# The last stage of a fused attention and mixture kernel: A and B formed by halves of the columns, and a new layout of the work around it

## The chip, the cores and the metric

One core of one Trainium2 chip runs the whole kernel as one program. The metric is device time in microseconds (us), the median over runs of the same kernel. A core has TensorE (PE, matmuls; its weight loads are shown as PEld), VectorE (DVE), ScalarE (ACT), GpSimd (POOL) and SyncE (SP, which issues the DMAs here). Each engine works through its own queue in order and waits on semaphores.

## The reference

Causal attention gives x, a soft mixture of experts turns x into 32 slots, and the slots are combined per token with weights c. Then comes the last layer:

```python
def _moe2_ref(x, w_a, w_b, w_out):
    a = x @ w_a                     # x: 896 x 768, w_a, w_b: 768 x 1536
    b = x @ w_b
    return (a * b @ w_out)          # w_out: 1536 x 768
```

Since x = c @ slots, row i of a * b is a sum over pairs of slots (s, u) of c_s c_u times A_s * B_u, where A = slots @ w_a and B = slots @ w_b. The kernel forms the products of pairs of slots once (P), multiplies them with w_out (M), forms c_s c_u for all tokens (cc), and multiplies cc with M to get the output.

## The kernel before, in words

All work up to about 280 us is the same in both kernels. The pairs of slots are cut into five tiles of up to 128 pairs (`TILES`). Tiles 0 and 1 are done in earlier stages beside the experts, tile 4 (a small one, 16 pairs) is called M4. The last stage, when the last slots are known, does this:

- `fold_a`, `fold_b` (matmuls `fp`, copy `sT`) bring the new slots into place.
- `ab_chunk(q, c)` multiplies the slots with w_a (q = 0) or w_b (q = 1). One chunk is one sixth of the contraction for all 1536 columns, as four matmuls to four groups of 32 rows of one PSUM bank; `ab_copy` and `ab_turn` (ACT, three transposes on PE, ACT) bring the result into `abt`, with the 1536 columns as 12 blocks f of 128 partitions.
- `p_tile(k, ...)` makes P for pair tile k in cuts of 2 or 3 blocks f (`PCUTS`): `products` on DVE (`pt`, `pf`: two multiplications for each part of the tile and an addition), then `conv_p` splits the sum into a high half (ACT) and a low half (DVE). Each product needs A and B of its block.
- `w_late` splits blocks of w_out into high and low halves in the same way (`whl`; ACT and DVE); four blocks, f = 8 to 11, are left from the stage before (`wt`).
- `m_late(k)` is 12 blocks of six matmuls each (`m_mats`, tiles `M`), in the order of `FLATE`, for tiles 2 and 3. `m_split` splits the result (`ml` for tiles 0 and 1, `mhl` for 2 and 3).
- `m4_mats`, `m4_copy`, `m4_fold` (tiles `M4`, `mc`, `M4f`, `m`) do tile 4.
- `cc_step(n, k)` forms cc for 256 tokens n and one or two pair tiles: matmuls `c` on PE, ACT copy and DVE multiplication (`gt`), ACT rounding and a subtraction on POOL (`cc`).
- `o_mats(t, k)` are the output matmuls (tiles `o`) of 128 tokens t with pair tile k; `o_store` copies and sends them.

The order on each engine is the order in which the program issues the instructions. The table `TAIL` sets it: after each unit of the stage, and after each block of `m_late` and each `o_mats`, `gap()` takes so many units from the queues W (`w_late`), S (`m_split`), P (products), C (`cc_step`) and X (M4) as the table has at that spot. What a later step needs and the table has not taken yet is taken just ahead of it. In the kernel before the products can be taken only when `turned` is set, after the whole stage:

```python
for i, u in enumerate(stage()):
    u()
    gap()
turned.append(1)
gap()
```

Of the kernel before, what the change touches and what calls it, by code (L numbers as in the profile page):

```python
# [19 lines left out]
S = 448  # L20
# [7 lines left out]
for _i in range(7):  # L28
# [62 lines left out]
def moe_kernel(ctx: ExitStack, tc: tile.TileContext, pk, vt, phi, w1, w2, wab, wo, rsel, out):  # L91
# [413 lines left out]
    with tc.manual_schedule():  # L505
# [262 lines left out]
        abt = r2.tile([128, 2, 12, NSLOT], F32, name="abt")  # L768
# [18 lines left out]
        def ab_turn(q):  # L787
            ps = psM.tile([128, 3, 4, NSLOT], F32, tag="m", name=f"abt{q}")
            for j in range(3):
                nc.tensor.transpose(  # L790
                    ps[:, j].rearrange("p g s -> p (g s)"), ab_sb[q][:, 128 * j:128 * j + 128], ident
                )
            nc.scalar.activation(
                out=abt[:, q].rearrange("p (g j) s -> p j g s", j=3), in_=ps, func=AF.Copy
            )
# [3 lines left out]
        def products(p, k, lo, w):  # L799
            f = slice(lo, lo + w)  # L800
            jobs = []
            off = 0
            for kind, *v in TILES[k]:
                if kind == "rect":
                    i, n, u, m = v
                    jobs.append((off, (n, m), [
                        (abt[:, q, f, i:i + n].unsqueeze(3).to_broadcast([128, w, n, m]),
                         abt[:, 1 - q, f, u:u + m].unsqueeze(2).to_broadcast([128, w, n, m])) for q in range(2)
                    ]))
                    off += n * m  # L810
                elif kind == "tri":
                    e, n = v
                    g = [abt[:, q, f].rearrange("p f (e r) -> p f e r", r=4)[:, :, e:e + n] for q in range(2)]
                    for r in (1, 2, 3):
                        jobs.append((off, (n, r), [
                            (g[q][:, :, :, r:r + 1].to_broadcast([128, w, n, r]), g[1 - q][:, :, :, 0:r])
                            for q in range(2)
                        ]))
                        off += n * r
                else:  # L820
                    i, n = v
                    jobs.append((off, (n, 1), [
                        (abt[:, 0, f, i:i + n].unsqueeze(3), abt[:, 1, f, i:i + n].unsqueeze(3))
                    ]))
# [21 lines left out]
        def p_tile(k, place, cuts, rot=0):  # L846
# [6 lines left out]
            at = [(rot + sum(cuts[:i])) % 12 for i in range(len(cuts))]  # L853
# [11 lines left out]

            q = [lambda: prod(0), lambda: conv_p(0), lambda: prod(1)]
# [93 lines left out]
        def m4_mats(h):  # L960
            if h == 0:
                mx[0] = two("so", "M4")
            for f0 in (0, 4, 8):
                for g in range(4):
                    f = f0 + g
                    nc.tensor.matmul(
                        mx[0][h][32 * g:32 * g + 32, 0:384], lhsT=mx["p"][:, f, :],
                        rhs=wo_sb[f // 2][:, f % 2, 384 * h:384 * h + 384],
                        start=(f < 4), stop=(f >= 8), skip_group_check=True,
                    )  # L970
# [30 lines left out]

        cu = combine_units()
# [16 lines left out]
        def w_late(j):  # L1019
            f, h = divmod(j, 2)  # L1020
            if h == 0 and f < 4:
                whl[f] = slot_tile(f"r{f}", F32R, f"whl{f}").rearrange("p (h q d) -> p h q d", h=2, q=2)
            elif h == 0 and f % 2 == 0:
                t = wabp.tile([128, 2, 2, 2, 384], F32R, tag=f"wab{f // 2 - 2}", bufs=1, name=f"whl{f}")
                whl[f], whl[f + 1] = t[:, 0], t[:, 1]
# [5 lines left out]
        def late_next():  # L1031
            if wl_j[0] < 16:
# [8 lines left out]
        def cc_step(n, k):  # L1041
# [18 lines left out]
            for q in range(2):  # L1060
                if n == 0:
                    ps = psA.tile([128, 2, 256], F32, tag=("so1", "so0")[q], name=f"c{q}_{n}_{k}")
                else:
                    ps = psM.tile([128, 2, 256], F32, tag="m", name=f"c{q}_{n}_{k}")
# [23 lines left out]
        def m_split(k):  # L1088
            if k < 2:
                if not mhl:  # L1090
# [17 lines left out]
        def p_next(k):  # L1108
            if not turned or (k == 3 and ptq[2]):
                return  # L1110
            if ptq[k] == [0]:
                ptq[k][:] = p_tile(k, ("t0", "t1") if k == 2 else "wab5", PCUTS[k], FLATE[0])
# [6 lines left out]
        def cc_next():  # L1119
            if ccq and (ccq[0][0] == 0 or done3 or ccq[0][0] == 1):  # L1120
# [12 lines left out]
        def split_next():  # L1133
            if splits:
                m_split(splits.pop(0))

        def gap():
            for name, take in (("W", late_next), ("S", split_next), ("P", p_any), ("C", cc_next), ("X", m4_next)):
                c = TAIL[name]
                for _ in range(c[spot[0]] if spot[0] < len(c) else 0):  # L1140
# [50 lines left out]
        def m_late(k):  # L1191
            for i, f in enumerate(FLATE):
                cuts = PCUTS[k]
                n = [c for c in range(len(cuts)) if sum(cuts[:c]) <= i][-1]
                while ptq[k] and (ptq[k] == [0] or len(ptq[k]) > p_left(k, n)):
                    p_any()
                if i == 0:
                    while k == 3 and len(m4_units) > 1:
                        m4_next()
                    mps[k] = two(("ab", "so")[k - 2], f"M{k}")  # L1200
                for h in range(2):
                    while f < 8 and wl_j[0] <= 2 * f + h:
                        late_next()
                    m_mats(k, i, f, h, whl[f][:, h, 0], whl[f][:, h, 1])
                gap()
# [5 lines left out]
        m_late(2)
        while len(m4_units) > 2:
            m4_next()
        m_split(2)
        m_late(3)
        done3.append(1)
# [82 lines left out]
```

## Time and profile before

| | us |
|---|---|
| median of three runs | 370.74 |
| lowest, highest run | 370.56, 374.9 |
| span of the profiled execution | 370.0 |

The profiled execution shows its own time only as the span, from its first to its last instruction; the median is 0.7 us above it. The last stage runs from about 280 us to the end. A timeline row merges instructions of one form; its length reaches from the first start to the last end, and matmuls overlap, so the pace is read from starts.

### The profile page before, as it was taken

To read this page: it belongs to the slowest core of one execution; us is meant where nothing else is said; L and a number is where in the kernel's file an instruction comes from. 1 tells how busy PE (TensorE), PEld (TensorE's weight loads), DVE (VectorE), ACT (ScalarE), POOL (GpSimd) and SP (SyncE) were. 2 spreads that over 40 slices of the span, in tenths; PEclk is the share of its full clock that TensorE was granted. 3 is DMA by queue.
4 is the path that set the end of the run, shared out by engine and by line. 5 is a ranking of instruction groups with operands and counts; after the bars stand their busy time and mean duration, and the time that the engine had idled before them with its cause. 6 is when DMAs were issued, how large, how long until landed. Compare 5 with 4: busy or idle time off the path is not lost.

```text
span 370.0 us, 6891 instructions
## 1 busy us (share of the span) xinstructions
PE 334.6 (90%) x2551; PEld 201.8 (55%) x2551; DVE 230.1 (62%) x620; ACT 202.0 (55%) x464; POOL 91.1 (25%) x128
## 2 busy tenths in 40 slices
PE   8897898989989978988988889999899889999996
PEld 5454454544544655343342346634565359899995
DVE  3689989999999962021025887507856669933121
ACT  2599999999999952103007445414546732422221
POOL 2457666667766510001000000000000110301110
PEclk9999989999999999999999989999999999999999
DMA  7677789998677787999999999778910000001222
GB/s 282 269 240 282 273 309 389 345 341 288 247 280 280 245 289 308 390 421 416 418 332 402 396 338 351 263 317 272 421 78 2 0 1 2 0 2 43 85 87 85
DMA packets 20224, 90.51 MB, mean 245 GB/s; under 512 B 2336, under 2 KB 5024, under 8 KB 20192
## 3 DMA queue, kind: packets, MB, share of 16 engines
q1 hardware_dynamic: 20192, 90.09, 65.2%
q8 instruction: 20, 0.33, 0.4%
q14 instruction: 12, 0.10, 0.1%
HBM read 87.33 MB, written 2.75 MB: 243 GB/s over the span
## 4 chain that ended last, share of the span: by engine, by line
PE 46%; ACT 27%; DVE 16%; issue 4%; DMA 3%; POOL 3%; ACTq 0%; POOLq 0%; DVEq 0%
ACT p L278 8%; PE o L1172 8%; PE M L891 8%; PE h L651 5%; PE so L692 4%; ACT raw L165 4%; PE ab L777 4%; ACT wab L164 4%; DVE pf L833 3%; ACT pT L314 3%; PE s L257 3%; DVE pt L832 3%; DMA raw<-in_wo_dram 3%; POOL p L294 3%; ACT wo L164 2%
## 5 line engine op out<-in xcount | busy, mean ns | idle before, releaser
L294 POOL TENSOR_SCALAR p<-p,rc 128x448 f32<-128x448 f32 (+6 forms) x84 | 69.2, 837 | 46.4 <-DVE rc L291 36.9
L257 PE MATMUL s<-qk 64*64 64x448 f32 (+6 forms) x336 | 48.5, 403 | 0.1
L1076 POOL TENSOR_TENSOR cc<-gt,cc 128x512 fp32r<-128x512 f32 (+1 forms) x6 | 6.9, 1156 | 157.6 <-ACT cc L1075 157.6
L278 ACT ACTIVATE p<-s,nm 128x448 f32<-128x448 f32 (+6 forms) x84 | 40.0, 492 | 7.8 <-DVE nm L268 7.6
L891 PE MATMUL M<-wt,P_t 128*128 128x384 f32 x168 | 35.9, 356 | 4.1 <-DVE P_t L864 1.3
L307 PE MATMUL t<-ident,p 128*128 128x128 f32 x192 | 33.7, 293 | 5.1 <-POOL p L294 5.1
L195 DVE SCALAR_TENSOR_TENSOR raw<-raw 128x768 int32<-128x768 int32 x36 | 35.2, 978 | 3.0 <-ACT raw L165 3.0
L263 DVE TENSOR_REDUCE nm<-s 128x1 f32<-128x448 f32 (+6 forms) x84 | 31.7, 411 | 8.0 <-PE s L257 8.0
L891 PEld LDWEIGHTS M<-wt,P_t 128*128 128x128 f32 x168 | 29.1, 193 | 13.6 <-ACT wt L885 4.8
L345 PE MATMUL v<-pT,v 128*64 128x448 f32 (+3 forms) x192 | 26.9, 396 | 7.9 <-ACT pT L314 7.7
L165 ACT ACTIVATE raw<-raw 128x768 int32<-128x768 uint32 x36 | 33.9, 941 | 0.0
L651 PE MATMUL h<-w,sT 128*32 128x512 f32 x192 | 29.9, 614 | 3.2 <-DMA w<-in_w_dram 2.3
L257 PEld LDWEIGHTS s<-qk 64*64 64x64 f32 x336 | 19.9, 136 | 21.3 <-issue 15.6
L307 PEld LDWEIGHTS t<-ident,p 128*128 128x128 f32 x192 | 20.7, 142 | 17.6 <-POOL p L294 7.3
L885 ACT ACTIVATE wt<-wo 128x384 fp32r<-128x384 f32 x48 | 21.8, 513 | 13.6 <-PE M L891 13.1
L886 DVE TENSOR_TENSOR wt<-wo,wt 128x384 fp32r<-128x384 f32 x48 | 23.8, 552 | 8.5 <-ACT wt L885 8.5
L198 DVE SCALAR_TENSOR_TENSOR wab<-wab,raw 128x768 int32<-128x768 int32 x24 | 27.9, 1162 | 0.8
L777 PE MATMUL ab<-wab,sT 128*32 128x384 f32 x288 | 27.5, 498 | 0.5 <-DVE sT L616 0.5
L692 PE MATMUL so<-w,hpad 128*32 128x384 f32 x256 | 24.8, 493 | 0.9 <-ACT wt L885 0.4
L314 ACT ACTIVATE pT<-t 128x512 f32<-128x512 f32 x35 | 21.7, 619 | 5.5 <-PE t L307 5.0
L345 PEld LDWEIGHTS v<-pT,v 128*64 128x64 f32 (+1 forms) x192 | 10.9, 134 | 22.6 <-ACT pT L314 14.0
L164 ACT ACTIVATE wab<-raw 128x768 f32<-128x768 f32 x24 | 23.1, 962 | 0.0
(155 smaller groups left out, 519.5 us busy)
## 6 DMA issues: line engine op xcount, KB each, us to landing
w<-in_w_dram SPq DMA_DIRECT2D x64, 768.0 KB, 8.0
raw<-in_wab_dram SPq DMA_DIRECT2D x24, 768.0 KB, 5.3
raw<-in_wo_dram SPq DMA_DIRECT2D x12, 768.0 KB, 4.4
qk<-in_pk_dram SPq DMA_DIRECT2D x12, 448.0 KB, 4.9
v<-in_pk_dram SPq DMA_DIRECT2D x12, 192.0 KB, 5.5
out_dram<-ost SPq DMA_DIRECT2D x6, 384.0 KB, 2.3
v<-in_vt_dram SPq DMA_DIRECT2D x12, 32.0 KB, 5.3
out_dram<-ost SPq DMA_DIRECT2D x2, 192.0 KB, 1.9
```

The lines of the kernel that those rows point to most:

```text
L164: nc.scalar.activation(out=dst, in_=hi, func=AF.Copy, scale=2.0 ** -112)
L165: nc.scalar.activation(out=pr[:, :, 0], in_=lw, func=AF.Copy, scale=2.0 ** -29, bias=-0.49999)
L195: nc.vector.scalar_tensor_tensor(out=b, in0=ph, scalar=-0x80000000, in1=b, op0=ALU.bitwise_and, op1=ALU.bitwise_or)
L257: nc.tensor.matmul(sb[r, o:o + n], lhsT=qT[r, 64 * i:64 * i + 64], rhs=kT[r, 0:n], start=False, stop=True, skip_group_check=True,)
L278: nc.scalar.activation(out=d["p"][:, POFF[i]:POFF[i] + n], in_=sb[:, o:o + n], func=AF.Exp, bias=d["nm"][:, c:c + 1], scale=d["scale"], ac ...
L294: nc.gpsimd.tensor_scalar(out=p[:, POFF[i]:POFF[i] + n], in0=p[:, POFF[i]:POFF[i] + n], scalar1=rc[:, CIX[i]:CIX[i] + 1], scalar2=1.0, op0 ...
L307: nc.tensor.transpose(ps[:, j, :], d["p"][:, o:o + 128], ident)
L345: nc.tensor.matmul(ps[r, 128 * kt:S], lhsT=lhsT, rhs=rhs, start=(kt == 0), stop=(kt == 3), skip_group_check=True)
L651: nc.tensor.matmul(ps[32 * g:32 * g + 32, :], lhsT=sT[:, 0, c, :], rhs=wt[8 * e + i // 3][:, 512 * (i % 3):512 * (i % 3) + 512], start=(i ...
L692: nc.tensor.matmul(so[32 * g:32 * g + 32, 0:384], lhsT=t[:, c, :], rhs=wt[8 * e + 4 + i // 4][:, 384 * (i % 4):384 * (i % 4) + 384], start ...
L777: nc.tensor.matmul(abps[q][32 * g:32 * g + 32, 0:384], lhsT=sT[:, 1, c, :], rhs=w[:, c % 2, 384 * g:384 * g + 384], start=(c == 0), stop=( ...
L891: nc.tensor.matmul(mps[k][h][:, 0:384], lhsT=l[:, f, :], rhs=r, start=(n == 0 and i == 0), stop=(n == 11 and i == 2))
```

## The change

A and B are no longer formed one after the other. `half_chunk(x, c)` multiplies one sixth of the contraction with 768 columns of both w_a and w_b (four matmuls, the same number and shape as before); half x = 0 covers blocks f = 6 to 11, half 1 blocks 0 to 5. Each half has its own copy and turn, and `turned` counts them. Products of tile 2 for blocks 6 to 11 may be taken after the first turn, the others after the second. `abt` now has A and B side by side for each block f. Two blocks of M of tile 2 (`AHEAD = 2`) are issued ahead of the second turn. M of tile 2 uses other PSUM banks. `TAIL` is now a table by spot; the steps C come later (from spot 36), M4 is cut into eight units. The two first `o_mats` (`EARLY`) no longer come ahead of M of tile 2.

```diff
-FLATE = (8, 9, 10, 11, 0, 1, 2, 3, 4, 5, 6, 7)
-EARLY = (0, 1)
+PROT = {2: (8, 10, 6, 0, 3), 3: (8, 11, 6, 0, 3)}
+FLATE = (8, 9, 10, 11, 6, 7, 0, 1, 2, 3, 4, 5)
+LORD = (6, 7, 0, 1, 2, 3, 4, 5)
+HALVES = (2, 0)
+AHEAD = 2
...
+    "C": {36: 1, 39: 1, 41: 1, 43: 1, 46: 1, 49: 1, 53: 1, 56: 1, 59: 1, 62: 1, 65: 1, 68: 1},
...
-        abt = r2.tile([128, 2, 12, NSLOT], F32, name="abt")
+        abt = r2.tile([128, 12, 2, NSLOT], F32, name="abt")
+        av = [abt[:, :, q, :] for q in range(2)]
...
+        def half_chunk(x, c):
+            nchunk[0] += x
+            if c == 0:
+                abps[x] = psA.tile([128, 512], F32, tag=f"ab{x}", name=f"ab{x}")
+            for gg in range(2):
+                g = HALVES[x] + gg
+                for q in range(2):
+                    r = 32 * (2 * gg + q)
+                    nc.tensor.matmul(
+                        abps[x][r:r + 32, 0:384], lhsT=sT[:, 1, c, :],
+                        rhs=wab_sb[3 * q + c // 2][:, c % 2, 384 * g:384 * g + 384],
+                        start=(c == 0), stop=(c == 5), skip_group_check=True,
+                    )
...
+        def last_stage():
+            q = [lambda: fold_a(so[:, 0:384], 1), lambda: fold_b(1)]
+            q += [(lambda c=c: half_chunk(0, c)) for c in range(6)]
+            q += [lambda: ab_copy(0), lambda: half_chunk(1, 0), lambda: (half_turn(0), turned.append(1))]
+            q += [(lambda c=c: half_chunk(1, c)) for c in range(1, 6)]
+            q += [lambda: ab_copy(1), lambda: (half_turn(1), turned.append(1))]
+            return q
...
-            if not turned or (k == 3 and ptq[2]):
+            if not turned or (k == 3 and ptq[2]) or (len(turned) < 2 and len(ptq[k]) == 4):
...
-        for i, u in enumerate(stage()):
+        last = last_stage()
+        last[-1:-1] = [lambda i=i: m_late(2, i) for i in range(AHEAD)]
+        for u in last:
             u()
             gap()
...
-        for k in EARLY:
-            o_mats(0, k)
```

What moves is seen best in the order on the engines. First PE, from the last chunks of A and B (`ab`) to the first blocks of M of tile 2. Before:

```order
L777 MATMUL ab_3045<-wab_112,sT 32x384 x4
L1067 MATMUL c_0_0_3099<-cst,rs 128x256 [waits PE_49,Activation_49]
...
L1067 MATMUL c_0_1_3109<-cst,rs 128x256 [waits Activation_49]
...
L1067 MATMUL c_0_1_3112<-cst,rs 128x256 [waits DVE_49]
...
L983 MATMUL M4f_3124<-mc,sel_97 96x384
L777 MATMUL ab_3045<-wab_113,sT 32x384 x8
L1067 MATMUL c_0_2_3138<-cst,rs 128x256 [waits Activation_49]
...
L790 MATMUL abt_3146<-ident,absb_3136 128x128 [waits DVE_49,Activation_49]
...
L1172 MATMUL o_0_3151<-ml,cc_3094 128x384
...
L891 MATMUL M_0_3177<-wt_8_2903,P_t_3165 128x384 [waits Activation_49]
L891 MATMUL M_0_3177<-wt_8_2903,P_t_3166 128x384 [waits DVE_49]
```

And now:

```order
L999 MATMUL M_1_2973<-wo_2216,p_2704 32x384 x2
L811 MATMUL ab_3029<-wab_110,sT 32x384
...
L925 MATMUL M_0_3125<-wt_8_2903,P_t_3039 128x384 [waits Activation_49]
L925 MATMUL M_0_3125<-wt_8_2903,P_t_3040 128x384 [waits DVE_49]
...
L925 MATMUL M_1_3126<-wt_9_2926,P_t_3040 128x384
L925 MATMUL M_1_3126<-wt_9_2926,P_t_3039 128x384
L820 MATMUL abt_3139<-ident,absb_3119 128x128 [waits Activation_49]
L820 MATMUL abt_3139<-ident,absb_3119 128x128 x2
L925 MATMUL M_0_3125<-wt_10_2941,P_t_3039 128x384
L925 MATMUL M_0_3125<-wt_10_2941,P_t_3040 128x384 [waits DVE_49]
```

The `c` and `o` matmuls have left this place; the second turn (`abt`) stands after two blocks of M.

On DVE, from the copy `sT` to the first products (`pt`). Before:

```order
L616 COPY sT<-fp_2972 128x3x2x32 [waits PE_49]
L886 TENSOR_TENSOR whl_3000<-wo_1316,whl_3000 128x384 [waits DMAHW3_49,DMAHW7_49,DMAHW1_49,Activation_49]
...
L886 TENSOR_TENSOR whl_3052<-wo_1555,whl_3052 128x384 [waits Activation_49] x4
L1100 TENSOR_TENSOR ml<-mq,ml 128x384 [waits Activation_49] x2
L1072 TENSOR_TENSOR gt<-gt,c_0_0_3102 128x512 [waits PE_49,Activation_49]
L1072 TENSOR_TENSOR gt<-gt,c_0_1_3112 128x512 [waits PE_49,Activation_49]
L987 TENSOR_TENSOR m_3119<-M4f_3120,m_3119 32x384 [waits Activation_49]
L987 TENSOR_TENSOR m_3119<-M4f_3124,m_3119 32x384 [waits Activation_49]
L1072 TENSOR_TENSOR gt<-gt,c_0_2_3140 128x256 [waits PE_49,Activation_49]
L1082 TENSOR_TENSOR cc_3094<-gt,cc_3094 32x256 [waits Activation_49]
L832 TENSOR_TENSOR pt<-abt 128x2x96 [waits Activation_49]
```

And now:

```order
L619 COPY sT<-fp_2967 128x3x2x32 [waits PE_49]
L920 TENSOR_TENSOR whl_2983<-wo_1555,whl_2983 128x384 [waits DMAHW2_49,DMAHW6_49,DMAHW0_49,Activation_49]
...
L920 TENSOR_TENSOR whl_3006<-wo_1316,whl_3006 128x384 [waits Activation_49]
L863 TENSOR_TENSOR pt<-abt 128x2x96 [waits Activation_49]
...
L895 TENSOR_TENSOR P_t_3040<-pf_3041,P_t_3039 128x256 [waits Activation_49] x2
L920 TENSOR_TENSOR whl_3093<-wo_1381,whl_3093 128x384 [waits Activation_49] x4
L920 TENSOR_TENSOR whl_3114<-wo_1462,whl_3114 128x384 [waits Activation_49] x4
L863 TENSOR_TENSOR pt<-abt 128x3x96 [waits Activation_49]
```

Eight subtractions of `whl` now stand ahead of the first products and eight behind the first three cuts; `ml`, `gt` and `m` come later.

On ACT, around the second copy of A and B (`absb`). Before:

```order
L986 ACTIVATE m_3119<-M4f_3120 96x384 [waits PE_49]
L986 ACTIVATE m_3119<-M4f_3124 96x384 [waits PE_49]
L784 ACTIVATE absb_3136<-ab_3045 128x384 [waits PE_49]
L1071 ACTIVATE gt<-c_0_2_3138 128x256 [waits PE_49]
L1080 ACTIVATE cc_3094<-gt 96x256 [waits DVE_49]
L793 ACTIVATE abt<-abt_3146 128x3x4x32 [waits PE_49]
L863 ACTIVATE P_t_3165<-pf_3167 128x256 [waits DVE_49] x3
```

And now:

```order
L894 ACTIVATE P_t_3039<-pf_3041 128x256 [waits DVE_49] x3
L919 ACTIVATE whl_3093<-wo_1381 128x384 [waits PE_49]
L919 ACTIVATE whl_3093<-wo_1381 128x384 x3
L919 ACTIVATE whl_3114<-wo_1462 128x384 [waits PE_49]
L919 ACTIVATE whl_3114<-wo_1462 128x384
L788 ACTIVATE absb_3119<-ab_3029 128x384 [waits PE_49,Activation_49]
L919 ACTIVATE whl_3114<-wo_1462 128x384 x2
L823 ACTIVATE abt<-abt_3139 128x3x2x64 [waits PE_49]
```

Six roundings of `whl` stand between the third cut's rounding (`P_t`) and `absb`, and two between `absb` and the copy into `abt`.

## Rows read from the trace of the kernel before

**Rows 1.** Windows: stretch, length, busy us of PE, PEld, DVE, ACT, POOL; PE clock; DMA.

```profile
290.00:330.00 40.00, 36.73 (x203) 29.41 (x195) 28.60 (x103) 13.56 (x30) 5.47 (x4) 0.96 0.00 1
294.24:297.66 3.42, 3.42 (x16) 1.04 (x18) 1.79 (x3) 1.74 (x4) 2.39 (x2) 0.50 0.00 0
330.00:365.00 35.00, 35.00 (x197) 32.85 (x196) 9.26 (x19) 9.84 (x22) 4.04 (x4) 1.00 0.17 68
```

**Rows 2.** Timeline of PE: start us, length us, instructions [idle before, who ended it].

```profile
281.89 5.99 PE L777 MATMUL ab<-wab,sT 128*32 128x384 f32 x72
...
290.25 0.83 PE L777 MATMUL ab<-wab,sT 128*32 128x384 f32 x8
291.49 0.74 PE L1067 MATMUL c<-cst,rs 64*128 64x256 f32 x4 [0.41 <-ACT mc L975]
...
293.83 2.50 PE L983 MATMUL M4f<-mc,sel 128*96 128x384 f32 x4
...
299.04 0.55 PE L790 MATMUL abt<-ident,absb 128*128 128x128 f32 x3 [0.19 <-ACT absb L784]
299.34 2.34 PE L1172 MATMUL o<-ml,cc 128*128 128x384 f32 x12
302.47 2.81 PE L891 MATMUL M<-wt,P_t 128*128 128x384 f32 x13 [0.79 <-ACT P_t L863]
305.75 2.18 PE L891 MATMUL M<-wt,P_t 128*128 128x384 f32 x11 [0.47 <-DVE P_t L864]
307.76 4.33 PE L891 MATMUL M<-whl,P_t 128*128 128x384 f32 x24
...
312.68 3.39 PE L891 MATMUL M<-whl,P_t 128*128 128x384 f32 x18
316.01 0.50 PE L1067 MATMUL c<-cst,rs 64*128 64x256 f32 x2
...
317.44 1.31 PE L891 MATMUL M<-whl,P_t 128*128 128x384 f32 x6
318.60 4.34 PE L891 MATMUL M<-wt,P 128*128 128x384 f32 x24
322.78 2.42 PE L891 MATMUL M<-whl,P 128*128 128x384 f32 x13
325.41 4.28 PE L891 MATMUL M<-whl,P 128*128 128x384 f32 x23 [0.21 <-DVE P L864]
```

**Rows 3.** Chain that ended last, 300 to 308 us: start, length, what.

```profile
300.63 0.36 DVE pt L832
...
302.87 0.27 DVE pt L832
...
304.12 0.27 DVE pt L832
...
305.69 0.37 DVE pt L832
...
307.33 0.34 DVE P_t L864
```

**Rows 4.** Timeline of POOL and DVE around 322 us.

```profile
321.65 1.60 POOL L1076 TENSOR_TENSOR cc<-gt,cc 128x512 fp32r<-128x512 f32 x1 [2.62 <-ACT cc L1075]
...
321.98 1.30 DVE L832 TENSOR_TENSOR pt<-abt 128x18 f32<-128x18 f32 x1
```

**Rows 5.** Timeline of PE where the kind of matmul changes.

```profile
275.00 1.31 PE L891 MATMUL M<-wt,P_t 128*128 128x384 f32 x6
276.24 0.85 PE L692 MATMUL so<-w,hpad 128*32 128x384 f32 x8
```

**Rows 6.** Timeline of ACT and of DVE, 278 to 301 us.

```profile
279.81 3.40 ACT L885 ACTIVATE whl<-wo 128x384 fp32r<-128x384 f32 x8
...
300.07 0.47 ACT L793 ACTIVATE abt<-abt 128x384 f32<-128x384 f32 x1
...
281.57 4.29 DVE L886 TENSOR_TENSOR whl<-wo,whl 128x384 fp32r<-128x384 f32 x9
```

More of the change, by code (lines that the diff above doesn't have):

```diff
@@ L793, in ab_turn, with half_turn @@
             nc.scalar.activation(
-                out=abt[:, q].rearrange("p (g j) s -> p j g s", j=3), in_=ps, func=AF.Copy
+                out=av[q].rearrange("p (g j) s -> p j g s", j=3), in_=ps, func=AF.Copy
+            )
+        nchunk = [0]
+        def half_chunk(x, c):
[10 more added lines that the diff above has]
+                        start=(c == 0), stop=(c == 5), skip_group_check=True,
+                    )
+        def half_turn(x):
+            ps = psM.tile([128, 3, 2, 2 * NSLOT], F32, tag="m", name=f"abt{x}")
+            for j in range(3):
+                nc.tensor.transpose(
+                    ps[:, j].rearrange("p g s -> p (g s)"), ab_sb[x][:, 128 * j:128 * j + 128], ident
+                )
+            nc.scalar.activation(
+                out=abt[:, 3 * HALVES[x]:3 * HALVES[x] + 6].rearrange("p (g j) q s -> p j g (q s)", j=3),
+                in_=ps, func=AF.Copy,
             )
@@ L812, in products @@
                     e, n = v
-                    g = [abt[:, q, f].rearrange("p f (e r) -> p f e r", r=4)[:, :, e:e + n] for q in range(2)]
+                    g = [av[q][:, f].rearrange("p f (e r) -> p f e r", r=4)[:, :, e:e + n] for q in range(2)]
                     for r in (1, 2, 3):
@@ L852, in p_tile @@
             ptl[k] = t
-            at = [(rot + sum(cuts[:i])) % 12 for i in range(len(cuts))]
+            at = PROT.get(k) or [sum(cuts[:i]) for i in range(len(cuts))]
             assert all(a + c <= 12 for a, c in zip(at, cuts))
@@ L958, in p4_make, with m4_mats @@
             products(mx["p"], 4, 0, 12)
-        def m4_mats(h):
-            if h == 0:
+        def m4_mats(h, f0):
+            if (h, f0) == (0, 0):
                 mx[0] = two("so", "M4")
[L963 to L970, printed above, removed]
+            for g in range(4):
+                f = f0 + g
+                nc.tensor.matmul(
+                    mx[0][h][32 * g:32 * g + 32, 0:384], lhsT=mx["p"][:, f, :],
+                    rhs=wo_sb[f // 2][:, f % 2, 384 * h:384 * h + 384],
+                    start=(f < 4), stop=(f >= 8), skip_group_check=True,
+                )
         def m4_copy():
@@ L1019, in w_late @@
         def w_late(j):
[L1020 to L1025, printed above, removed]
+            i, h = divmod(j, 2)
+            f = LORD[i]
+            if h == 0 and i < 4:
+                whl[f] = slot_tile(f"r{i}", F32R, f"whl{f}").rearrange("p (h q d) -> p h q d", h=2, q=2)
+            elif h == 0 and i % 2 == 0:
+                t = wabp.tile([128, 2, 2, 2, 384], F32R, tag=f"wab{i // 2 - 2}", bufs=1, name=f"whl{f}")
+                whl[f], whl[LORD[i + 1]] = t[:, 0], t[:, 1]
             w = whl[f][:, h]
@@ L1060, in cc_step @@
             for q in range(2):
[L1061 to L1064, printed above, removed]
+                ps = psM.tile([128, 2, 256], F32, tag="m", name=f"c{q}_{n}_{k}")
                 ab.append(ps)
@@ L1089, in m_split @@
             if k < 2:
-                if not mhl:
+                if 0 not in mhl:
                     ml = wabp.tile([128, 2, 2, 768], F32R, tag="wab2", bufs=1, name="ml")
@@ L1133, in split_next @@
         def split_next():
-            if splits:
+            if splits and len(turned) > 1:
                 m_split(splits.pop(0))
@@ L1138, in gap, with m_late @@
             for name, take in (("W", late_next), ("S", split_next), ("P", p_any), ("C", cc_next), ("X", m4_next)):
-                c = TAIL[name]
-                for _ in range(c[spot[0]] if spot[0] < len(c) else 0):
+                for _ in range(TAIL[name].get(spot[0], 0)):
                     take()
             spot[0] += 1
-        for i, u in enumerate(stage()):
+        def m_late(k, i):
+            f = FLATE[i]
+            cuts = PCUTS[k]
+            n = [c for c in range(len(cuts)) if sum(cuts[:c]) <= i][-1]
+            while ptq[k] and (ptq[k] == [0] or len(ptq[k]) > p_left(k, n)):
+                p_any()
+            if i == 0:
+                while k == 3 and len(m4_units) > 1:
+                    m4_next()
+                mps[k] = two(("mm", "so")[k - 2], f"M{k}")
+            for h in range(2):
+                while f < 8 and wl_j[0] <= 2 * LORD.index(f) + h:
+                    late_next()
+                m_mats(k, i, f, h, whl[f][:, h, 0], whl[f][:, h, 1])
+        last = last_stage()
+        last[-1:-1] = [lambda i=i: m_late(2, i) for i in range(AHEAD)]
+        for u in last:
             u()
             gap()
-        turned.append(1)
-        gap()
         ops = {}
@@ L1189, in o_store @@
             nc.sync.dma_start(out=out[128 * t:128 * t + 128, d], in_=ost[:, d])
[L1191 to L1205, printed above, removed]
+        for i in range(AHEAD, 12):
+            m_late(2, i)
+            gap()
+        for i in range(12):
+            m_late(3, i)
+            gap()
+        done3.append(1)
         while splits:
             split_next()
-        for k in EARLY:
-            o_mats(0, k)
[L1211 to L1216, printed above, removed]
         m_split(3)
-        for t, k in ((0, 2), (1, 0), (1, 1), (1, 2), (0, 3), (0, 4), (1, 3), (1, 4)):
-            if t or k not in EARLY:
-                o_mats(t, k)
+        for t, k in ((0, 0), (0, 1), (0, 2), (1, 0), (1, 1), (1, 2), (0, 3), (0, 4), (1, 3), (1, 4)):
+            o_mats(t, k)
             if k == 4:
```

29 lines of the change are left out of this document (18 added, 11 removed), and 5 rows, old and new, of the table TAIL.

## The prediction

> **What bounds the kernel now.** I read the windows first. From 330 to 365 us PE is busy for all 35 us at full clock [rows 1]: the output matmuls run back to back, and the change leaves their number and shape alone. What it can save lies between 280 and 330, where PE waits or is slow. The timeline of PE shows where [rows 2]. For the pace: 24 matmuls of M take from 318.60 to 322.78, 0.174 each; 72 rows of `ab` take 5.99, 0.082 each with the end taken off. A `c` step of four matmuls inside a stream of M costs 0.74 (24 matmuls from 307.76 should end at 311.94, and M goes on at 312.68) and slows its surroundings by up to another 0.20 (18 matmuls from 312.68 should end at 315.81, the next `c` starts at 316.01); I take 0.84. With these, PE loses:
>
> - 290.25 to 293.83: eight rows of `ab` end at 290.91, then come two `c` steps that hang on ACT and DVE. 2.92 us pass where two steps cost 1.68: 1.24.
> - 294.24 to 297.66: the granted clock is 0.50 in this stretch, 1.2 of 2.4 GHz, with PE busy throughout [rows 1]: 3.42 us give 1.71 us of work, 1.71 lost. Ahead of it lie the waits of the first item.
> - 299.34 to 305.75: 12 `o` matmuls end at 301.43, M starts at 302.47; its 13 matmuls end at 304.73, the next comes at 305.75: 2.06.
> - 312.68 to 317.44: 1.63 us pass from the end of M's 18 matmuls to the next, a `c` step costs 0.84: 0.79.
> - 322.78 to 325.41: 13 matmuls should end at 325.04: 0.37.
>
> Together 6.17 us. The chain of waits says who sets this [rows 3]: from 300.63 it runs through `pt`, `pf` and their additions on DVE without a gap, and PE's waits at 302.47 and 305.75 end with ACT's and DVE's halves of P. The products can't start before the second turn, which ends late because of the first two items.
>
> **The change, part by part.** *First half.* The matmuls are as many and as wide. 24 rows ahead of 281.89 give 279.92 as the start of M4 in both kernels. Now 8 rows of M4 and 48 of the first half (4.6 us) bring PE to 284.5; its copy on ACT is hidden behind 16 rows (1.3 us). The turn's three transposes take 0.30 (299.04 to 299.34), its copy 0.47 [rows 2, 6]: DVE can start the products at about 286.8, 13.8 us earlier. DVE is free for that: the eight subtractions of `whl` ahead of them take 0.47 each (nine in 4.29 [rows 6]) from 280.4 and end at 284.2. PE's remaining rows, 48 of `ab` and 40 of M4 less the 16 named, cover DVE's first cuts until 292.1.
>
> *Products.* A cut of two blocks takes 1.25 (302.87 to 304.12), a cut of three 1.64 (305.69 to 307.33) [rows 3]. Three cuts of two and their low halves (0.34 each) are done at 291.8, so M's first blocks at 292.1 wait for nothing. Next DVE has eight more `whl` subtractions, to 295.6, and two cuts of three, to 298.9; the first one's low half is there at 299.4. PE, after two blocks of M (12 matmuls, 2.1 us), the turn, and four more blocks, wants it at 299.2: a wait of 0.2. If all DVE and ACT durations were 5% longer, this wait and one at the second turn would together be 1.0; I take 0.3, between 0 and 1.0.
>
> *The second turn* hangs on ACT: six roundings of `whl` stand ahead of `absb`. Eight take 3.40, 0.42 each [rows 6]. They start when the third cut's rounding is done, 291.2, and end at 293.8; `absb` at 294.2. PE has M until 294.2 to cover it; the cover is used up to 0.1 us. The two roundings behind `absb` run during the transposes.
>
> *Tile 3.* In the trace before DVE took from 307.33 to 325.41 for the rest of tile 2, tile 3, two `gt`, two `mhl` and the delay named below: 18.1 us, so tile 3 needs at most 13. It starts at 300.0 and its last piece is there by 313.2 at the latest; PE starts tile 3 at 307.2 and wants the last piece 54 matmuls and one `c` step later, at 317.5. The earlier cuts (by these durations due 2 to 4 us before PE wants them) have less slack, about 2.2 us at the least. So the losses at 312.68 and 322.78 go.
>
> *Steps C* move behind the products. Their price on PE is in the sum already (two steps at 0.84 and one short one, no longer beside waits). Their POOL subtraction did one more thing: a product of 18 elements on DVE that started at 321.98, beside POOL's 1.60 us, lasted 1.30, until POOL was done [rows 4], and about 1.1 us too long. That delay ends in the 0.37 of the last item; now POOL's first subtraction comes at about 317, after the last product.
>
> *What it adds.* M changes to another kind of matmul and back at two more places, the second turn and M4's fold. Six matmuls of M from 275.00 should end at 276.04, and the other kind starts at 276.24 [rows 5]: 0.20 out; the way back I bound by 0 and the same 0.20. So 0.4 to 0.8, I take 0.6. M4 in pieces between chunks of `ab` is the same kind of matmul; the bounds are 0 and 0.2, and I take 0. The new layout of `abt` doubles the stride between blocks in what DVE reads; bounds: a gain of 0, since the length of a row of products follows its elements already, and the loss that is a rival below; I take 0. The other PSUM banks for M are free since ACT's copies at 279.8; nothing is queued behind them. SP's queue is not touched until the stores.
>
> *Room as a page counts it.* From 290 to 330 PE shows 36.73 us of matmuls and 29.41 of weight loads, from 330 to 365 it shows 35.00 and 32.85 [rows 1]. By matmuls the first stretch has 3.27 us of idle time, and 1.71 from the clock, less than my 6.17, since a row's end lies over the start of a wait. The Trainium skill (Perfetto Trace Analysis, "Identifying the Most-Contended Engine") calls the busy share of matmuls a poor measure of how near TensorE is to its limit and takes that of weight loads instead. By that the stretch would need 29.41 / 0.94 = 31.3 us, and the gain could reach 8.7 us before what the change adds. It counts as room the rows of `ab`, `M4f` and `c`, whose loads are short and which follow each other without a wait [rows 2]; so I keep 6.17, and give the rest a rival.
>
> **Sum.** 6.17 − 0.3 − 0.6 = 5.3 us off the span of 370.0: 364.7. The runs' median is 0.7 above that span, so I set the gain against it: 370.74 − 5.3 = 365.4 us, 1.4% faster.
>
> **Rivals.**
>
> - *The clock falls again.* In the stretch where PE has no wait, from 330 to 365, the clock is 1.00 throughout [rows 1]; the fall came behind waits. With waits of at most 0.3 us there should be no fall in the new last stage; but the rows show only what went ahead of one fall. One such fall costs 1.7: 367.1. 12%.
> - *The loop DVE, ACT, PE, ACT, DVE is longer than drawn.* ACT's six roundings wait behind the third cut's rounding, `absb` behind them, the turn behind `absb`, DVE's fourth cut behind the turn; PE has 0.1 us to spare there and nothing else to do. Hand-offs that are 5 to 10% longer cost 0.8 to 1.5: 366.6. 12%.
> - *Slower: the products on DVE slow down with the new layout of `abt`.* Tiles 2 and 3 have about 16 us of them here (7.0 in tile 2's cuts, some 9 of tile 3's 13). Nearly every delay is passed on at the third and fourth cuts and at tile 3, so the change breaks even where products take about 0.35 longer per us, and at half as long again PE loses some 8 us: 370.74 − 5.3 + 8 = 373.4. Against it: the first products of two cuts at different blocks of `abt`, at 302.87 and 304.12, take the same 0.27 [rows 3]. 3%.
> - *It does not do what it says:* the products of the first half wait for both turns. Then PE's two blocks of M ahead of the second turn would wait for products that wait for this turn, and the program would stand still; so I give this no chance.
> - *More than the sum:* every wait gone, changes of kind free, and a little less for the `c` steps: 6.2 to 6.6, 364.3. 8%. Faster by over 2% means under 363.3, 7.4 us less; no wait in the rows is left for that.
> - By the page's measure of room, 8.7 less 0.9 would give 362.9; the traces bear it out only if `ab` and `c` could be made to load less, which the change doesn't do. I count 3 of the 8% for it.
>
> **How the numbers follow.** The forecast holds 65% (364.6 to 366.2, by the bounds of the waits 0 to 1.0 and the changes 0.4 to 0.8). The range takes in the full gain and one fall of the clock: 363.8 to 367.4. Two per cent, 7.4 us, is about what a measurement of this kernel can tell from no change. Faster by over 2% gets 0.06 and slower by over 2% 0.04 (the rival with 3%, and what I have not thought of), within 2% 0.90.
>
> **What would show it.** Right: the first `pt` of the last stage at about 287, PE without a wait above 0.3 us from 280 to the end, the clock at 1.00 from 280 on, the first matmul of tile 3 at about 307, the first `o` at about 322, the last matmul some 5.3 us earlier. Wrong: a wait of PE at the second turn (the loop), at the fourth cut or in tile 3 (DVE), products longer per element than before (layout), or a clock of 0.50 in any stretch after 280.

## The result, and the profile after

| | before | after |
|---|---|---|
| median, us | 370.65 | 365.88 |
| lowest, highest | 369.22, 374.9 | 364.8, 367.12 |
| profiled execution: span | 370.0 | 362.9 |
| last stage, first `fp` to last matmul | 86.94 | 81.22 |

The ratio is 0.9885 [0.9851, 0.9919]: 1.15% faster, and 4.8 us by the medians. That is within 2% of no change, but the interval leaves out 1, so less than the 2% of the prediction can be told here. The prediction was 365.4. Ratios and mean clocks, here and below, leave out executions over 1.5% above the fastest of their kernel: three of 74 of before, one of no_ahead, one of old_layout. The profiled execution of after took 365.3 us with a span of 362.9, so 2.4 us lie around the span, not 0.7.

I measure the last stage from the start of its first `fp` matmul to the start of the last matmul of the kernel. What comes ahead of it is the same in both kernels, but in these two executions it took 279.23 and 277.88. So times of after are to be read 1.35 later when they are set beside those of before. The windows of after, with the columns of [rows 1]:

```profile
277.88:290.00 12.12, 12.12 (x146) 5.29 (x149) 8.52 (x29) 5.95 (x15) 0.00 (x0) 1.00 0.01 2
290.00:330.00 40.00, 39.68 (x229) 35.76 (x218) 27.86 (x95) 18.06 (x40) 4.30 (x4) 1.00 0.00 1
```

PE is busy for 39.68 of 40 us where it was busy for 36.73 [rows 1], and the clock is 1.00. The Trainium skill (Perfetto Trace Analysis, "Identifying the Most-Contended Engine") takes the busy share of weight loads, beside the share of the peak FLOPs, as the measure of how near TensorE is to its limit. The trace differs here: with one wait of 0.32 left, the loads show 35.76, 89%, against 94% from 330 to 365 before, and so would still count some 2 us of room.

The timeline of PE in after, with the columns of [rows 2]:

```profile
277.88 0.78 PE L615 MATMUL fp<-sel,f_sb 128*128 128x64 f32 x6
...
284.53 0.55 PE L820 MATMUL abt<-ident,absb 128*128 128x128 f32 x3
...
289.55 1.47 PE L811 MATMUL ab<-wab,sT 128*32 128x384 f32 x16
290.95 2.35 PE L925 MATMUL M<-wt,P_t 128*128 128x384 f32 x12
293.15 0.55 PE L820 MATMUL abt<-ident,absb 128*128 128x128 f32 x3
293.46 2.33 PE L925 MATMUL M<-wt,P_t 128*128 128x384 f32 x12
295.62 2.42 PE L925 MATMUL M<-whl,P_t 128*128 128x384 f32 x13
298.36 3.22 PE L925 MATMUL M<-whl,P_t 128*128 128x384 f32 x17 [0.32 <-DVE P_t L895]
301.41 1.45 PE L1016 MATMUL M4f<-mc,sel 128*96 128x384 f32 x4
302.41 3.58 PE L925 MATMUL M<-whl,P_t 128*128 128x384 f32 x18
305.83 4.34 PE L925 MATMUL M<-wt,P 128*128 128x384 f32 x24
...
313.23 0.74 PE L1106 MATMUL c<-cst,rs 64*128 64x256 f32 x4
313.90 3.40 PE L925 MATMUL M<-whl,P 128*128 128x384 f32 x18
317.22 0.74 PE L1106 MATMUL c<-cst,rs 64*128 64x256 f32 x4
...
320.61 2.35 PE L1225 MATMUL o<-ml,cc 128*128 128x384 f32 x12
...
359.10 0.33 PE L1218 MATMUL o<-m,cc 96*128 96x384 f32 x1
```

A row with a bracket is a row that PE waited for. Of the rows shown in [rows 2] five have one; here it is one, `P_t` at 298.36, the fourth cut's low half that the prediction named. M of tile 2 starts at 290.95, straight behind the last rows of `ab`. In before it started at 302.47, with `o` and two waits around it.

DVE and ACT around the first and the second turn:

```profile
285.64 0.36 DVE L863 TENSOR_TENSOR pt<-abt 128x192 f32<-128x192 f32 x1 [2.79 <-ACT abt L823]
...
290.69 3.89 DVE L920 TENSOR_TENSOR whl<-wo,whl 128x384 fp32r<-128x384 f32 x8
294.49 0.45 DVE L863 TENSOR_TENSOR pt<-abt 128x288 f32<-128x288 f32 x1
...
290.15 2.58 ACT L919 ACTIVATE whl<-wo 128x384 fp32r<-128x384 f32 x6
292.63 0.47 ACT L788 ACTIVATE absb<-ab 128x384 f32<-128x384 f32 x1
```

The first product starts at 285.64, that is 287.0 on before's clock, where it started at 300.63 [rows 3]. `absb` ends at 293.10 and PE's turn starts at 293.15: the two blocks of M cover ACT's six roundings and `absb`, with nothing to spare.

### The profile page after: what moved, and what is told of

It reads as the page before. It is cut to its first block, busy times and chain, and to the rows that moved or that the text cites. A ratio compares the mean times of both kernels' runs of the same rounds, so it can differ in the third digit from the quotient of the medians.

```text
span 362.9 us, 6891 instructions
## 1 busy us (share of the span) xinstructions
PE 329.5 (91%) x2551; PEld 200.1 (55%) x2551; DVE 228.4 (63%) x620; ACT 202.0 (56%) x464; POOL 91.2 (25%) x128
## 4 chain that ended last, share of the span: by engine, by line
PE 49%; DVE 27%; ACT 16%; DMA 3%; issue 3%; POOL 1%; ACTq 0%; POOLq 0%; DVEq 0%
PE M L925 11%; PE o L1225 9%; PE h L654 5%; DVE raw L198 5%; PE so L695 4%; ACT p L281 4%; DVE wab L201 4%; DVE nm L266 4%; DMA raw<-in_wo_dram 3%; ACT raw L168 3%; ACT pT L317 2%; PE s L260 2%; DVE pf L864 2%; PE ab L781 2%; DVE pt L863 2%
## 5 line engine op out<-in xcount | busy, mean ns | idle before, releaser
L297 POOL TENSOR_SCALAR p<-p,rc 128x448 f32<-128x448 f32 (+6 forms) x84 | 70.2, 850 | 42.4 <-DVE rc L294 37.9
L260 PE MATMUL s<-qk 64*64 64x448 f32 (+6 forms) x336 | 46.9, 391 | 0.9 <-DMA qk<-in_pk_dram 0.9
L1111 DVE TENSOR_TENSOR gt<-gt,c 128x512 f32<-128x512 f32 (+2 forms) x12 | 6.5, 544 | 25.6 <-ACT gt L1110 25.6
```

Source lines behind the costliest of these rows:

```text
L260: nc.tensor.matmul(sb[r, o:o + n], lhsT=qT[r, 64 * i:64 * i + 64], rhs=kT[r, 0:n], start=False, stop=True, skip_group_check=True,)
L297: nc.gpsimd.tensor_scalar(out=p[:, POFF[i]:POFF[i] + n], in0=p[:, POFF[i]:POFF[i] + n], scalar1=rc[:, CIX[i]:CIX[i] + 1], scalar2=1.0, op0 ...
```

## The experiments

Theory 1: the early products, covered on PE by the second half of A and B, bring the gain. Theory 2: the new places of the fillers bring it. Theory 3: it is the clock. All kernels, with the last stage of their one profiled execution, the median and the ratio to before in the same comparison:

| kernel | last stage | median | ratio |
|---|---|---|---|
| both_turns | 86.64 | 372.76 | 1.0057 [1.002, 1.0094] |
| no_ahead | 82.70 | 368.61 | 0.9957 [0.9924, 0.999] |
| old_c_late | 86.95 | 371.30 | 1.0052 [1.0022, 1.0082] |
| after_again | 81.21 | 366.29 | 0.9906 [0.9872, 0.9939] |
| old_keep | 85.99 | 371.24 | 1.0019 [0.9986, 1.0052] |
| old_layout | 85.31 | 370.58 | 0.9984 [0.9951, 1.0017] |
| c_beside | 88.81 | 372.95 | 1.0074 [1.0042, 1.0106] |
| order5 | 80.99 | 366.47 | 0.9875 [0.9825, 0.9926] |
| before_look1, before_look2 | 87.00, 86.87 | 374.99, 370.32 (one execution each) | |
| two_more_whl | 81.83 | 366.13 | 0.9885 [0.9846, 0.9925] |
| c_ml_first | 87.67 | 372.46 | 1.0046 [1.0009, 1.0083] |

**both_turns: no product until both turns are done.**

```diff
-            if not turned or (k == 3 and ptq[2]) or (len(turned) < 2 and len(ptq[k]) == 4):
+            if len(turned) < 2 or (k == 3 and ptq[2]):
...
-        last[-1:-1] = [lambda i=i: m_late(2, i) for i in range(AHEAD)]
+        last[-1:-1] = [lambda: None] * AHEAD
...
-        for i in range(AHEAD, 12):
+        for i in range(12):
             m_late(2, i)
-            gap()
+            if i >= AHEAD:
+                gap()
```

The products that stood at spots 10 to 12 of `TAIL` are taken at spot 19.

> A and B are formed by halves as in the changed kernel and the fillers stand where it has them, but no product is taken until both turns are done, and no block of M stands ahead of the second turn. I measure the last stage as the time from the first fp matmul behind 270 us to the last matmul of the kernel: 86.9 us before, 81.2 after. Theory 1 (the early products, covered by the second half, bring the gain): PE waits some 0.7 at the second turn, then 2.7 and 0.9 for the first products of tile 2; the last stage is about 85.0 if the clock stays at 1.00, 86.7 if it falls once behind these waits; the time 369.7 to 371.4. Theory 2 (the new places of the fillers bring it, the halves little): waits of at most 1.5 in all, last stage at most 82.7, time 365.9 to 367.4.

Its timeline of PE, and one window:

```profile
293.67 0.55 PE L820 MATMUL abt<-ident,absb 128*128 128x128 f32 x3 [0.67 <-ACT absb L788]
296.83 0.44 PE L925 MATMUL M<-wt,P_t 128*128 128x384 f32 x1 [2.61 <-ACT P_t L894]
297.96 5.82 PE L925 MATMUL M<-wt,P_t 128*128 128x384 f32 x23 [0.69 <-DVE P_t L895]
303.61 5.36 PE L925 MATMUL M<-whl,P_t 128*128 128x384 f32 x30
...
298.60:302.10 3.50, 3.50 (x13) 3.50 (x13) 3.35 (x13) 0.80 (x2) 0.00 (x0) 0.53 0.00 0
```

The waits come as theory 1 has them: 0.67, 2.61, 0.69. Then the clock is at half for some 3.4 us (0.53 in the window): 23 matmuls take 5.65 from start to start where 4.00 is the pace, 1.65 lost. Without that the last stage is 85.0, as expected, and all the rest of the new layout is worth 0.3 against before (85.3 at full clock, shown below). As the whole cause theory 2 falls. The time is 1.4 us above the range of theory 1; see the clock, below.

**no_ahead: the two blocks of M come behind the second turn.** The edit is the second and the third piece of the diff above.

> The changed kernel, but the two blocks of M that stand ahead of the second turn come behind it. Theory 1 (the loop DVE, ACT, PE, ACT: the second turn hangs behind the third cut's rounding and six whl roundings on ACT, and only these two blocks, 12 x 0.174 = 2.1, cover it): PE waits about 2.3 for absb; the wait of 0.3 at the fourth cut and the changes of kind (0.4) go; last stage about 83.0 at full clock, 84.7 with one fall of the clock; time 367.7 or 369.4. Theory 2 (fillers alone matter): last stage 81.2 to 81.8, time as after.

```profile
293.20 0.55 PE L820 MATMUL abt<-ident,absb 128*128 128x128 f32 x3 [2.12 <-ACT absb L788]
```

PE waits 2.12 and the last stage is 82.70, 1.5 longer than after. The clock stays at 1.00 in it, in spite of the wait. The loop through ACT is what the two blocks cover.

**old_c_late: before, with C steps and the early `o` behind M.**

```diff
-EARLY = (0, 1)
+EARLY = ()
...
-                if n == 0:
-                    ps = psA.tile([128, 2, 256], F32, tag=("so1", "so0")[q], name=f"c{q}_{n}_{k}")
-                else:
-                    ps = psM.tile([128, 2, 256], F32, tag="m", name=f"c{q}_{n}_{k}")
+                ps = psM.tile([128, 2, 256], F32, tag="m", name=f"c{q}_{n}_{k}")
```

In `TAIL`, C gets the places of the changed kernel (one spot later, since the stage has one less after it), and the other queues close the gap of two spots that the early `o` leave.

> The kernel before, with A and B one after the other and all products behind the second turn, but the first C steps moved behind the products and the two early o blocks behind M, as the changed kernel has them. Theory 1: the waits around the c steps go (1.24 at 290 to 294, 0.79 and 0.37 later), but with the 12 o matmuls the cover of the first products goes too (2.1 us), so that PE waits 0.7 at the second turn and some 3.3 for the first cuts; last stage about 84.4 at full clock and 86.1 if it falls once; time 368.2 to 370. Theory 2 (the fillers' new places bring the gain): last stage at most 82.5, time 367 or less.

```profile
290.08 1.53 PE L983 MATMUL M4f<-mc,sel 128*96 128x384 f32 x4
291.54 0.85 PE L777 MATMUL ab<-wab,sT 128*32 128x384 f32 x8
293.06 0.55 PE L790 MATMUL abt<-ident,absb 128*128 128x128 f32 x3 [0.67 <-ACT absb L784]
296.00 7.17 PE L891 MATMUL M<-wt,P_t 128*128 128x384 f32 x24 [2.40 <-ACT P_t L863]
303.01 8.49 PE L891 MATMUL M<-whl,P_t 128*128 128x384 f32 x48
...
295.00:302.00 7.00, 6.00 (x19) 5.83 (x20) 6.52 (x27) 1.78 (x4) 0.00 (x0) 0.51 0.00 0
```

With C and `o` gone from there, PE waits for the products instead: 0.67 and 2.40, where I had 0.7 and 3.3. From 295 us, while PE still waits, the clock is 0.51 over 7 us; 24 matmuls take 7.01 instead of 4.18, 2.83 lost. At full clock the last stage would be 84.1, 1.2 better than before, so the fillers' places do give something. The time is no better, and above the 370 that theory 1 allowed: in this execution the clock took 2.83 in the last stage, not 1.7.

**after_again.** The changed kernel unchanged.

> The changed kernel once more. Theory 1: no fall of the clock in the last stage, which has no wait above 0.3; last stage 81.2 plus or minus 0.3, whatever falls come earlier; time 365 to 367. Theory 3 (the falls come anywhere, whatever PE did ahead of them): a fall in the last stage is as likely as elsewhere, and one would make it 82.9.

81.21, clock 1.00 throughout the last stage; two neighbouring falls came earlier, from 168.5 to 176 us (clock 0.55 there), and one at 33 to 36 us.

**old_layout: before with only `abt`'s layout changed.**

```diff
-        abt = r2.tile([128, 2, 12, NSLOT], F32, name="abt")
+        abt = r2.tile([128, 12, 2, NSLOT], F32, name="abt")
+        av = [abt[:, :, q, :] for q in range(2)]
```

Reads and writes of `abt[:, q]` become `av[q]`.

> The kernel before with only the layout of abt changed: A and B of a block side by side. Theory 1: DVE's products take what they took (0.27 for two blocks, 0.37 for three), PE waits as before, last stage 86.9 with one fall of the clock and 85.2 without; time as before. Rival (the new layout slows the products): products longer by a third or more, the last stage longer by 2 us or more.

```profile
289.61 0.73 PE L1068 MATMUL c<-cst,rs 64*128 64x256 f32 x4 [0.41 <-ACT mc L976]
...
291.95 1.53 PE L984 MATMUL M4f<-mc,sel 128*96 128x384 f32 x4
293.41 1.50 PE L778 MATMUL ab<-wab,sT 128*32 128x384 f32 x16
...
298.95 2.81 PE L892 MATMUL M<-wt,P_t 128*128 128x384 f32 x13 [0.77 <-ACT P_t L864]
...
290.00:301.00 11.00, 9.36 (x54) 6.14 (x54) 6.64 (x21) 5.44 (x12) 2.55 (x2) 1.00 0.00 1
```

The waits are those of [rows 2] within 0.02. On DVE a cut of two blocks takes 1.24 and one of three 1.63, where [rows 3] give 1.25 and 1.64, and the median is that of before: the layout costs nothing. This execution had no fall of the clock in the last stage, so it shows what before takes at full clock: 85.31. In before `M4f` and the 16 rows behind it took 2.42 and 2.10 at the low clock, from 293.83 [rows 2] to 296.25 and on to 298.35; here 1.46 and 1.43. That is 1.63 less, the whole difference of the two last stages. So the same waits were followed by a fall in one execution and not in the other.

**before_look1, before_look2.** Two more executions of before.

> The kernel before, unchanged, for its clock. The kernel before with the other layout had the same waits and no fall of the clock in its last stage (85.3), so my term of 1.71 may come in some executions alone. Theory 1 as predicted (the fall belongs to the waits): a fall between 290 and 300 again, last stage 86.9. Theory 1b (waits make a fall possible, not certain): one or no fall, last stage 86.9 or 85.3.

> The kernel before, unchanged, once more: as for the first look; two more executions without a fall would mean that the typical gain of the last stage is 85.3 less 81.2, that is 4.1, and not 5.7.

Both had a fall there: in the second the clock is 0.53 from 291.9 to 295.5, last stage 86.87. With the first profile that is three of three, and none of one with the other layout.

**old_keep: dummy matmuls in before's first waits.**

```diff
             ab = []
+            if n == 0 and k < 2:
+                keep(idle2(), (9, 12)[k])
             for q in range(2):
+                if (n, k, q) == (0, 1, 1):
+                    keep(idle2(), 8)
```

`idle2()` is a PSUM bank that is free there.

> The kernel before, with dummy matmuls (ident16 by ident16, 128 columns, into a bank that nobody reads, about 0.056 each) in the three waits of PE ahead of and between the first c steps: 9, 12 and 8 of them. They add nothing to the output and should end before what PE waits for. Theory 1 (the fall of the clock from 294 comes from PE's waits right ahead of it): the clock stays at 1.00 there and the last stage is 85.2 instead of 86.9; time 1.7 less than before. Theory 3 (a fall comes in the last stage whatever PE does ahead of it): a clock of 0.50 for some 3.4 us again, last stage 86.9 plus or minus 0.3.

```profile
294.18 0.68 PE L324 MATMUL idle<-ident 128*128 128x128 bf16 x9
294.78 0.74 PE L1078 MATMUL c<-cst,rs 64*128 64x256 f32 x4
...
297.63 1.53 PE L983 MATMUL M4f<-mc,sel 128*96 128x384 f32 x4
...
304.63 2.83 PE L891 MATMUL M<-wt,P_t 128*128 128x384 f32 x13 [0.79 <-ACT P_t L863]
```

The `c` rows have no bracket any more and the clock is 1.00 in the last stage, but the dummies overran the waits by 0.6 to 0.7 (first `c` to `M4f` 2.85 against 2.34 [rows 2], and 0.12 ahead of it): 85.99. The times are those of before. Since one execution without a fall is no proof (old_layout had none either), this is inconclusive for the single fall; what it shows is that filling these waits bought no time. With some 0.65 of work added, a saving of 1.7 would have left 1.0 less, 0.9972 of before, which lies outside [0.9986, 1.0052].

**c_beside and c_ml_first: C steps back beside the products.** The second also takes `ml` first.

```diff
-    "C": {36: 1, 39: 1, 41: 1, 43: 1, 46: 1, 49: 1, 53: 1, ...
+    "C": {29: 1, 31: 1, 33: 1, 35: 1, 37: 1, 39: 1, 53: 1, ...
...
-    "S": {33: 1, 35: 1, 38: 1},
+    "S": {26: 1, 28: 1, 33: 1},
...
-        splits = [2, 0, 1]
+        splits = [0, 1, 2]
```

The last two pieces are those of the second.

> The changed kernel, but the first six C steps come from spot 29 on at every second spot, that is, right behind M of tile 2 and beside the products of tile 3, instead of from spot 36. Theory 1 (the steps cost only their 0.84 when nothing hangs on them, and much more beside products, since ACT and DVE do both): PE waits some 2.9, 0.7 and 0.7 at c steps, last stage about 85.5 at full clock and 87.2 with one fall; time 370 or more. Rival (their place matters little): last stage 81.2 to 82.0, time as after.

> As the changed kernel with the first six C steps from spot 29 on, but the splits of tiles 0 and 1 (ml) come first, at spots 26 and 28, so that the place of gt, which held the source of ml, is free before the C steps. With ml behind the products, PE had waited 4.95 for ACT's gt, and ACT for DVE's ml. Theory 1 (C steps beside products wait for DVE, whatever stands ahead): PE waits some 2.7 and 0.75 at the second and third c step for DVE's gt, which stands behind tile 3's products; last stage about 84.6 at full clock; time 369 or more. Rival (that cost was the place of ml alone): waits of under 0.6 in all, last stage 81.2 to 82.0.

PE in the first, and ACT and DVE, which it waits for:

```profile
315.91 1.52 PE L1106 MATMUL c<-cst,rs 64*128 64x256 f32 x4 [4.95 <-ACT gt L1110]
317.35 4.12 PE L925 MATMUL M<-wt,P 128*128 128x384 f32 x12
...
315.26 0.60 ACT L1110 ACTIVATE gt<-c 128x512 f32<-128x512 f32 x1 [5.09 <-DVE ml L1139]
...
313.21 1.95 DVE L1139 TENSOR_TENSOR ml<-mq,ml 128x384 fp32r<-128x384 f32 x4
```

And PE in the second:

```profile
307.71 0.97 PE L1106 MATMUL c<-cst,rs 64*128 64x256 f32 x4 [0.49 <-DVE m L1020]
...
311.84 0.50 PE L1106 MATMUL c<-cst,rs 64*128 64x256 f32 x2 [0.88 <-ACT gt L1110]
314.12 0.79 PE L1106 MATMUL c<-cst,rs 64*128 64x256 f32 x2 [1.78 <-DVE gt L1111]
314.84 4.21 PE L925 MATMUL M<-wt,P 128*128 128x384 f32 x12
```

In the first the wait is one of 4.95 where I had three of 4.3 in sum, and its cause is one that I had not drawn: `gt` lies where the source of `ml` lay, and DVE has `ml` behind tile 3's products. The second takes that away; 0.49 (for DVE's `m`), 0.88 (for ACT's `gt`) and 1.78 remain at the C steps, 3.2 us in all, the last since DVE's `gt` stands behind products. In both the clock falls while PE still waits, at about 314.4 and 313.3 us (12 matmuls of M take 4.06 and 4.14 instead of 2.09), and both are slower than before, by 0.7 and 0.5%. So where the C steps stand matters much: beside products they undo the whole gain.

**two_more_whl: eight roundings ahead of `absb`, not six.**

```diff
-    "W": {2: 2, 3: 2, 4: 4, 13: 2, 14: 2, 15: 2, 16: 2},
+    "W": {2: 2, 3: 2, 4: 4, 13: 2, 14: 2, 15: 4},
```

> The changed kernel with eight whl roundings on ACT ahead of the second absb instead of six. Theory 1 (the two blocks of M cover the second turn with 0.1 us or less to spare): PE waits 0.7 to 0.8 for absb, two roundings at 0.42 less the spare; the wait of 0.33 at the fourth cut stays or shrinks by what the turn's delay gives ACT and DVE; last stage 81.7 to 82.0. Rival (there is more slack than the order shows): no wait at the turn, last stage 81.2.

```profile
292.06 2.35 PE L925 MATMUL M<-wt,P_t 128*128 128x384 f32 x12
295.08 0.55 PE L820 MATMUL abt<-ident,absb 128*128 128x128 f32 x3 [0.68 <-ACT absb L788]
```

The bracket shows 0.68 of the two roundings' 0.83. By starts it is more: the turn comes 3.02 behind the first block of M, where in after it came 2.20 behind it (290.95 to 293.15), so 0.82 reaches PE and there was next to no spare. The last stage is 0.61 longer, since the wait at the fourth cut shrinks by 0.21; the times can't tell it from after.

**order5: the fourth cut's low half ahead of the fifth cut.**

```diff
-                order = "p0 p1 c0 p2 c1 c2 p3 p4 c3 c4".split()
+                order = "p0 p1 c0 p2 c1 c2 p3 c3 p4 c4".split()
```

> The changed kernel with one thing moved: the low half of tile 2's fourth cut comes ahead of the fifth cut's products on DVE (p3 c3 p4 c4 instead of p3 p4 c3 c4). Theory 1: the one wait left in the last stage, 0.33 of PE for P_t, goes; last stage 81.0, 0.2 less than after, which the times can't tell apart. Rival: DVE waits for ACT's rounding between the two cuts and is late with the fifth cut; a new wait of 0.3 to 0.6 there, last stage 81.3 to 81.6.

```profile
296.84 5.36 PE L925 MATMUL M<-whl,P_t 128*128 128x384 f32 x30
...
298.01 0.56 DVE L895 TENSOR_TENSOR P_t<-pf,P_t 128x384 fp32r<-128x384 f32 x1 [0.59 <-ACT P_t L894]
...
313.12 0.82 PEld L925 LDWEIGHTS M<-whl,P 128*128 128x128 f32 x5 [0.36 <-DVE P L895]
```

The 30 matmuls follow each other without a wait and take 5.20 to the next `M4f` (302.04), where after takes 5.79. But DVE now waits 0.59 for ACT's rounding ahead of the low half, as the rival had it. It is late from there on, not with the fifth cut but with tile 3's fourth, for which the weight loads wait (last line): the 18 matmuls around it take 3.56 instead of 3.22. So 0.59 is gained and 0.34 given back, 80.99, 0.2 less. It is the best version here, by the profile; the medians of 366.47 and 366.29 can't tell.

## Why the prediction was right

- *Products start early.* Right: first `pt` at 287.0 on before's clock, M of tile 2 without a wait, tile 3 at 307.2 (305.83 and 1.35), first `o` at 322.0. Undone together with the two blocks of M ahead of the second turn, which can't stand there without it (both_turns), it costs 3.8 of the 4.1 us that the last stage gains at full clock (85.0 against 81.2); the two blocks undone alone (no_ahead) cost 1.5.
- *The second turn's loop.* Right to 0.1: covered, with next to nothing to spare (0.82 of 0.83 came through in two_more_whl).
- *Wait at the fourth cut.* I took 0.3. The bracket says 0.32; by the pace from starts, by which the sum counts its waits, it was 0.48 (13 matmuls from 295.62 should end at 297.88, the next came at 298.36).
- *Tile 3 and C steps.* Right: no wait, though the slack at tile 3's fourth cut was about 1.4 and not 2.2 (in order5 that cut came 1.1 later, PE 0.6 sooner, and the wait was 0.36). A `c` step of four costs 0.86 (0.67 to the next M, and 18 matmuls behind it take 3.32 instead of 3.13); I had 0.84.
- *Changes of kind and M4.* Mis-sized, 0.6 given back. The second turn costs 0.18 more than its transposes (0.11 ahead, which holds what PE waited for `absb`, and 0.07 behind). At `M4f` it is 0.09 ahead and 0.29 behind, but `M4f` itself takes 1.00 between blocks of M (301.41 to 302.41) where it took 1.46 between rows of `ab` (old_layout, and 1.46 in old_c_late). Net some 0.1, not 0.6.
- *The clock, 1.71 in the sum.* This is the term that failed. It was read rightly from the one profiled execution: that fall is gone, and the last stage gained 5.72 there, against 5.3. But it was set against a median. The 71 executions of before in these comparisons have a mean granted clock of 0.9891, the 14 of after 0.9901. (1 − clock) x span, an estimate of what the clock took, is 4.0 and 3.6 us. So by it the clock is worth 0.4 (0.6 over all 74), not 1.7. Why after still loses 3.6 is open: the profiles don't show that the falls moved, since ahead of the last stage the three of before have two, four and one, those of after and after_again one and three. Executions with a clock of 0.995 have a median span of 367.0 before (12) and 362.8 after (6), those of 0.984 to 0.987 368.9 (28) and 364.4 (5): 4.2 and 4.5 less at equal clock, close to the 4.1 of the last stage at full clock. The estimate counts every fall alike, and that is rough. From 0.995 to the lower group it has 3.3 us more, but the spans are only 1.9 and 1.6 longer, while the fall in the last stage cost its full 1.63 (old_layout).
- *Span against median.* I put 0.7 around the span. It is 2.2 in before; the profiled execution of before had lost some 5.5 us to the clock (0.985), against 4.0 in the mean, and its span of 370.0 lies 1.6 above the median span of 368.4. As I took the gain from the median, this did no harm.

By terms, the sum at full clock was 6.17 − 1.71 − 0.9 = 3.6; measured 85.3 − 81.2 = 4.1. The difference is the price of the changes of kind (0.5 less), the wait at the fourth cut (0.2 more) and 0.19 that before lost at its second turn (299.04 in [rows 2]) and the sum left out. With 0.4 for the clock that makes 4.5, between the medians' 4.8 and 4.1. The clock term was too large and the rest of the gain too small; they offset each other in part, and that 365.4 came so close to 365.88 is partly luck.

Theory 1 holds, with a part for theory 2: the fillers' places alone give 1.2 at full clock (old_c_late), but leave a wait, and in the profiled execution the clock took it back; only with early products is there work to stand in their place. Theory 3 in its plain form, that the falls explain the gain, is refuted by the executions at equal clock and by the last stages at full clock (85.3 against 81.2).

## What to carry to other kernels

Where a stage must be complete before the next engine can start, cut it so that the next engine can begin at the first part, and check by the queue of every engine in the loop what covers it: here two blocks of M cover six roundings and a copy with next to nothing to spare. A filler is only free if what it waits for is not queued behind the critical work, buffers included. And a loss to the clock that one profile shows is not to be booked in full against a median.

## What was not expected of the hardware

Four kernels whose longest wait of PE was 1.8 to 5 us ran at a lower mean clock over all their executions: both_turns 0.9825 (8), old_c_late 0.9835 (6), c_beside 0.9847 (10), c_ml_first 0.9806 (10), against 0.9891 in before and 0.9901 in after. None of those 34 executions reached 0.994; 13 of 71 and 6 of 14 did. In each of the four profiles the clock was at half, for some 3.4 us in both_turns and some 6.8 in the others. In those three it fell 0.8 to 1.5 us before PE went on (at 295.0 us in old_c_late, where M starts at 296.00), in both_turns after PE had gone on. no_ahead, with one wait of 2.12, had no fall in its profiled last stage and a mean of 0.9871 (9), and old_layout had none with the waits of before. So here the kernels with long waits lost more to the clock, and a wait need not bring a fall. What decides it is left open, and so is why the falls ahead of the last stage (in the profiles at about 13, 33, 45, 79, 170, 194, 213 and 262 us) come in some executions and not in others. Dummy matmuls did not raise the mean (old_keep 0.9881).
